# Layer two of a routed pair of expert layers: gathers before the branch, eight weight pieces in flight, three routing rounds

## The chip, the core and the metric

The program runs on one core of a Trainium2 chip. Its compute engines are TensorE (PE, matrix products, whose weight loads the profile lists as PEld), VectorE (DVE), ScalarE (ACT) and GpSimd (POOL); SyncE (SP) issues most DMAs. Each engine works through its own queue in order, and semaphores join the queues. The metric is the device time of one execution in microseconds. The kernel before took 804.73 us, the median of three runs (803.93 to 805.32).

## The reference

Attention with decay gives 2304 tokens of 512 numbers, which pass through two expert layers. In layer one each token goes to its best expert. In layer two the experts fill up: the pairs of token and expert are taken in falling order of their score, and each expert holds exactly 2304 / 8 = 288 tokens.

```python
def _moe2_ref(x, w_gate, w1, w2):
    N, D = x.shape
    E = w_gate.shape[1]
    cap = N // E
    logits = x @ w_gate
    flat = logits.flatten()
    order = np.argsort(-flat)
    assigned = -np.ones(N, dtype=np.int64)
    counts = np.zeros(E, dtype=np.int64)
    for idx in order:
        tok, e = (int(idx) // E, int(idx) % E)
        if assigned[tok] >= 0 or counts[e] >= cap:
            continue
        assigned[tok] = e
        counts[e] += 1
    out = np.zeros((N, D), dtype=np.float32)
    for e in range(E):
        mask = assigned == e
        h = np.maximum(x[mask] @ w1[e], 0.0)
        out[mask] = h @ w2[e]
    return out

def reference(**kwargs):
    ...
    x = attn_out.transpose(0, 2, 1, 3).reshape(B * S, H * D)
    x = _moe_ref(x=x, **moe_kwargs)
    return _moe2_ref(x=x, **moe2_kwargs)
```

## The kernel before

The program is written out in the order in which each engine runs it. Attention comes first, then layer one, its eight experts in falling order of their token counts, then the routing of layer two and its eight experts.

A weight matrix of an expert comes in pieces of 128 x 1024 numbers: pieces 0 to 3 belong to the first product, 4 to 7 to the second. `load` (L853) has SP fetch a piece into a raw tile `wraw`. `upper` (L860) has ACT write its high half `whi`, `lower` (L867) has DVE subtract and write the low half `wlo`, and `split` does both. Products are sums of three: high by high, high by low, low by high. There are four `wraw` buffers, so a fifth load waits until `lower` has read the oldest. `load_next` takes the next piece of the list of all 128.

`Experts.all` (L1624) runs an expert's first product in eight steps (L1574, eight groups of twelve matmuls), its second in four (L1598), and puts other work beside each step in `beside`: the splits of the pieces of the next expert, the gather of its rows (`fetch`, one indirect DMA of POOL per 128 tokens), their transposition (`columns`) and the results of the expert before. A group's sum lies in one of two banks named `pl`; ACT writes its positive part as `room_hh` and DVE the rest as `room_hl` (L1577, L1578), and then the bank is free. The first expert of a layer has nobody before it to prepare its own later pieces, so it splits pieces 4 to 7 in its own steps 0 to 3 (`LATE`).

The class `First` starts the first expert of layer one while attention ends. DVE sorts the experts by their counts in `order_all`, nine short instructions that end with the tile `ordi`, which tells SP which expert's weights to load next.

The class `Clear` routes layer two. Each of the eight experts has a threshold in `c_T`. In a round (L1378) every token chooses the expert with the best score among those whose threshold it passes (`choose`, mask `c_oh`), the margins `c_z` are compared with a grid of 128 steps (`c_cmp`, L1390), twenty matmuls count for each step how many tokens of each expert lie above it (L1395), and the threshold rises by the largest step that leaves 288 (L1396 to L1400). Three rounds run beside the last expert of layer one, on the tokens known by then, dealt out over its steps by the table `SPEC`. Four more run when all scores are there. Then `place` (L1411) turns the choice into the index list `ix`, and computes a flag that is 1 if an expert has not exactly 288 tokens. `run` (L1465) branches on the flag: if it is 1, four more rounds and another placing follow, and if that fails too an exact search. In the traced execution the branch is not taken. After it come the gathers of expert 0, the low halves of its first four pieces with four loads, ten warm-up matmuls, and the transposes (`first_columns`, with matmuls at L890).

Of the kernel before, what the change touches and what calls it, by code (L numbers as in the profile page):

```python
# [289 lines left out]
def attention(tc, ctx, qkT, vrow, vT, f, emb, x_d, identf, identb, psum, R, tau, first_expert):  # L290
# [524 lines left out]
    nc.vector.tensor_reduce(ut, u.rearrange("p k e t -> p e t k"), axis=AX.X, op=ALU.add)  # L815
    for _ in R.order_all():
        pass
    first_expert.last_rows(work)
    first_expert.split(3)
# [26 lines left out]
class Weights:  # L846
# [6 lines left out]
    def load(self, p, j):  # L853
        raw = self.pool.tile([128, 1024], F32, name="wraw", bufs=4)
        e = self.expert(p)
        src = self.w1 if j < 4 else self.w2
        self.nc.sync.dma_start(raw, src[bass.ds(e, 1), j % 4].rearrange("o p x -> (o p) x"))
        self.raw[p, j] = raw

    def upper(self, key, j):  # L860
        pool, k, bufs = (self.pool, "1", 4) if j < 4 else (self.pool2, "2", 8)
        hi = pool.tile([128, 1024], F32R, name="whi" + k, bufs=bufs)
        lo = pool.tile([128, 1024], F32R, name="wlo" + k, bufs=bufs)
        self.nc.scalar.activation(hi, self.raw[key, j], AF.Copy)  # L864
        self.parts[key, j] = (hi, lo)
# [370 lines left out]
ROUNDS = (4, 4)  # L1236

SPEC = {0: 1, 2: 1, 4: 1, 6: 1, 7: 1, 7.5: 5, 9: 1, 9.5: 5, 11: 1, 12: 1}


class Clear:
# [7 lines left out]
    def __init__(self, tc, R, const, work, psum, up, y_d):  # L1249
# [6 lines left out]
        self.oh = self.ohz[:, :, 1:]  # L1256
# [103 lines left out]
    def choose(self, last=False):  # L1360
# [12 lines left out]
        yield  # L1373
        for c in CUT:
            TT(self.oh.rearrange("p e c -> p c e")[:, c], self.V[:, c],
               self.mn[:, c, None].to_broadcast([128, c.stop - c.start, E]), op=ALU.is_equal)

    def round(self, tag="py"):  # L1378
        nc, TT = self.nc, self.nc.vector.tensor_tensor
        yield from self.choose()  # L1380
        ohc = self.oh.rearrange("p e c -> p c e")
        for c in CUT:
            TT(self.V[:, c], ohc[:, c], self.Rm[:, c], op=ALU.mult)
# [3 lines left out]
        h = (0, 14, NCP)  # L1387
# [6 lines left out]
        for c in range(NC3):  # L1394
            nc.tensor.matmul(p, self.cmp[:, :, c], self.oh[:, :, c], start=(c == 0), stop=(c == NC3 - 1))  # L1395
# [18 lines left out]
    def place(self, ix2):  # L1414
# [47 lines left out]
        nc.vector.tensor_scalar(ix2, ut, -1.0, None, op0=ALU.add)  # L1462
        return again[0]

    def run(self, ix2):  # L1465
# [11 lines left out]
        with tc.If(self.place(ix2) > 0):  # L1477
            go(ROUNDS[1])
            with tc.If(self.place(ix2) > 0):
# [6 lines left out]
                self.place(ix2)  # L1486


class Experts:
# [134 lines left out]
    def all(self, load_next, after, extra):  # L1624
# [3 lines left out]
        for p in range(E):  # L1628
# [4 lines left out]
            def beside(step, p=p):  # L1633
# [3 lines left out]
                elif step < 8:  # L1637
# [4 lines left out]
                    if p == 0 and step in LATE:  # L1642
                        W.split(0, 4 + LATE.index(step))
# [10 lines left out]
                elif nW is not None and not last:  # L1654
# [4 lines left out]
        if not self.second:  # L1659
            self.finish(lambda: extra(E - 1, 12))  # L1660

# [18 lines left out]
def moe(tc, ctx, psum, R, later, ut, first_expert, W1, W2, load_next, x_d, wg, out, identf):  # L1680
# [121 lines left out]
    C.run(ix2)  # L1802

    def gather2(p, t, w):
        g = work.tile([128, YW], F32, name="xg", bufs=4)
# [13 lines left out]
    L2.fetch(0)  # L1819
# [84 lines left out]
```

## Time and profile before

| | |
|---|---|
| median of three runs | 804.73 us |
| profiled execution | 805.88 us |
| its span, first to last instruction | 803.7 us |
| busy: PE, PEld, DVE, ACT, POOL | 741.7, 711.0, 498.0, 408.3, 303.3 us |
| mean granted clock of PE | 0.957 |

The profiled execution is a run of its own, and its span leaves out what lies before the first instruction and after the last. Busy times of different engines overlap, so they say which engine is nearly full and not what bounds a stage. The page also cuts the span into 40 slices of 20 us: PE is at 90% or more in all but the first two, four between about 502 and 583 us, and the last. A clock of 1.00 is 2.4 GHz, 0.50 is 1.2 GHz.

### The profile page before, as it was taken

To read this page: it belongs to the slowest core of one execution; us is meant where nothing else is said; L and a number is where in the kernel's file an instruction comes from. 1 tells how busy PE (TensorE), PEld (TensorE's weight loads), DVE (VectorE), ACT (ScalarE), POOL (GpSimd) and SP (SyncE) were. 2 spreads that over 40 slices of the span, in tenths; PEclk is the share of its full clock that TensorE was granted. 3 is DMA by queue.
4 is the path that set the end of the run, shared out by engine and by line. 5 is a ranking of instruction groups with operands and counts; after the bars stand their busy time and mean duration, and the time that the engine had idled before them with its cause. 6 is when DMAs were issued, how large, how long until landed. Compare 5 with 4: busy or idle time off the path is not lost. (4 is left out here: it accounts for less than half of the span.)

```text
span 803.7 us, 16338 instructions
## 1 busy us (share of the span) xinstructions
PE 741.7 (92%) x5813; PEld 711.0 (88%) x5813; DVE 498.0 (62%) x1314; ACT 408.3 (51%) x898; POOL 303.3 (38%) x674
## 2 busy tenths in 40 slices
PE   3799999999999999999999999845899999999995
PEld 1499999999898899999999999723799999999993
DVE  5666887877887676555466567673555555655530
ACT  3456666767657455455555556100555555555420
POOL 5587767777663446423123111004021222232011
PEclk9799999999999999999999999855899999999998
DMA  5456766767664556455565562004546655665310
GB/s 124 92 122 153 168 152 164 161 157 174 143 198 131 170 175 194 149 182 175 168 192 180 185 183 84 26 1 168 174 171 197 211 171 195 209 194 175 124 37 31
DMA packets 70254, 121.74 MB, mean 151 GB/s; under 512 B 29498, under 2 KB 38714, under 8 KB 70164
## 3 DMA queue, kind: packets, MB, share of 16 engines
q1 hardware_dynamic: 63924, 101.24, 45.5%
q0 software_dynamic: 6240, 19.36, 6.4%
q8 instruction: 50, 0.82, 0.4%
q14 instruction: 40, 0.33, 0.1%
HBM read 96.46 MB, written 14.63 MB: 138 GB/s over the span
## 5 line engine op out<-in xcount | busy, mean ns | idle before, releaser
L870 DVE TENSOR_TENSOR wlo<-wraw,whi 128x1024 fp32r<-128x1024 f32 x128 | 156.3, 1227 | 126.4 <-ACT whi L864 122.0
L864 ACT ACTIVATE whi<-wraw 128x1024 fp32r<-128x1024 f32 x128 | 134.6, 1056 | 3.6 <-DMA wraw<-v 3.2
L477 POOL TENSOR_TENSOR opB<-raw,opA 64x576 fp32r<-64x576 f32 x64 | 90.7, 1417 | 34.3 <-ACT opA L473 31.6
L1577 ACT ACTIVATE room_hh<-pl 128x288 fp32r<-128x288 f32 (+8 forms) x128 | 51.9, 406 | 97.9 <-PE pl L1574 94.4
L1574 PE MATMUL pl<-room_xh,whi 128*128 128x288 f32 (+7 forms) x512 | 94.9, 308 | 4.5 <-DVE room_hl L1578 4.4
L1574 PE MATMUL pl<-room_xl,whi 128*128 128x288 f32 (+7 forms) x512 | 90.6, 299 | 0.0
L1574 PE MATMUL pl<-room_xh,wlo 128*128 128x288 f32 (+7 forms) x512 | 90.5, 299 | 0.0
L1598 PE MATMUL py<-room_hh,wlo 128*128 128x288 f32 (+7 forms) x480 | 89.8, 310 | 0.0
L1578 DVE SCALAR_TENSOR_TENSOR room_hl<-pl,room_hh 128x288 fp32r<-128x288 f32 (+8 forms) x128 | 57.3, 448 | 52.0 <-ACT room_hh L1577 50.4
L1574 PEld LDWEIGHTS pl<-room_xh,whi 128*128 128x128 f32 x512 | 76.4, 192 | 6.1 <-DVE room_hl L1578 5.6
L1574 PEld LDWEIGHTS pl<-room_xl,whi 128*128 128x128 f32 x512 | 76.8, 191 | 0.0
L1574 PEld LDWEIGHTS pl<-room_xh,wlo 128*128 128x128 f32 x512 | 76.7, 191 | 0.0
L1806 POOL DMA_INDIRECT xg<-y_d,ix x24 | 29.2, 1219 | 125.2 <-PE px L1514 89.9
L1598 PE MATMUL py<-room_hh,whi 128*128 128x288 f32 (+7 forms) x480 | 75.9, 300 | 0.0
L1598 PE MATMUL py<-room_hl,whi 128*128 128x288 f32 (+7 forms) x480 | 75.8, 300 | 0.0
L513 PE MATMUL pl<-opA 96*128 96x288 f32 (+2 forms) x192 | 67.5, 356 | 7.0 <-DVE opA L382 3.7
L549 PE MATMUL px<-opA 128*128 128x288 f32 (+2 forms) x192 | 72.2, 376 | 0.0
L1598 PEld LDWEIGHTS py<-room_hh,wlo 128*128 128x128 f32 x480 | 70.5, 189 | 0.0
L582 PE MATMUL py<-vv,room_hh 128*128 128x73 f32 x480 | 69.7, 265 | 0.4 <-DVE vv L497 0.4
L517 DVE CUSTOM_DVE_ANT_0 mxs<-pl,mask 128x512 f32<-128x512 f32 (+3 forms) x128 | 61.9, 484 | 13.1 <-PE pl L513 9.7
L1598 PEld LDWEIGHTS py<-room_hl,whi 128*128 128x128 f32 x480 | 69.1, 188 | 0.0
L1598 PEld LDWEIGHTS py<-room_hh,whi 128*128 128x128 f32 x480 | 69.0, 189 | 0.0
(367 smaller groups left out, 1417.4 us busy)
## 6 DMA issues: line engine op xcount, KB each, us to landing
wraw<-w SPq DMA_DIRECT2D x64, 512.0 KB, 4.1
wraw<-v SPq DMA_DIRECT2D x64, 512.0 KB, 3.5
raw<-qkT SPq DMA_DIRECT2D x32, 288.0 KB, 4.3
opB<-opA SPq DMA_DIRECT2D x64, 144.0 KB, 3.1
vv<-vrow SPq DMA_DIRECT2D x32, 160.0 KB, 4.6
vt<-vT SPq DMA_DIRECT2D x16, 288.0 KB, 4.4
x_d<-xr SPq DMA_DIRECT2D x16, 256.0 KB, 2.7
opA<-chl SPq DMA_DIRECT2D x60, 2.2 KB, 1.8
```

The source lines that it names most:

```text
L477: nc.gpsimd.tensor_tensor(b_[lo, t, :], raw[:, t, :], r32(a[0:64, t, :]), op=ALU.subtract)
L513: nc.tensor.matmul(p[:, :wp], af[0:96, q0:q0 + 128], a[0:96, 1, k0:k0 + wp], start=True, stop=True)
L517: nc.vector.tensor_tensor_reduce(t[:qw, :w], p[:qw, :w], mask[:qw, m0:m0 + w], 1.0, part4[:qw] if i == 4 else -3.0e38, op0=ALU.add, op1=AL ...
L549: nc.tensor.matmul(o, af[:, ks], a[:, 0, q1 - wp:q1], start=True, stop=False)
L582: nc.tensor.matmul(p[:, i, :], PT[n % 2][0][:, c:c + 128], v_[:, j, :], start=(k == 0), stop=(k == len(AORD) - 1))
L864: self.nc.scalar.activation(hi, self.raw[key, j], AF.Copy)
L870: self.nc.vector.tensor_tensor(lo, self.raw.pop((key, j)), r32(hi), op=ALU.subtract)
L1574: nc.tensor.matmul(o, a[:, d, f0:f0 + 128], b[:, d, o0:C], start=(n == 0), stop=(n == 11))
L1577: nc.scalar.activation(hh[:, fc, c0:C], o, AF.Relu)
L1578: nc.vector.scalar_tensor_tensor(hl[:, fc, c0:C], o, 0.0, r32(hh[:, fc, c0:C]), op0=ALU.max, op1=ALU.subtract)
L1598: nc.tensor.matmul(o, a[:, fc, :], b[:, fc, :C], start=(n == 0), stop=(n == 23))
L1806: nc.gpsimd.indirect_dma_start(out=g[:w], out_offset=None, in_=y_d, in_offset=IOA(ap=ix2[:w, p * NT + t:p * NT + t + 1], axis=0))
```

## The change

Five things change.

The first expert's fourth piece is split ahead of `order_all` and not behind it.

Pieces 4 to 7 get raw buffers of their own, four tiles `wraw2`, so eight pieces can be on their way. Their high and low tiles go from eight buffers to six. The first expert of layer one calls `load_next` twice in each of its steps 0 to 3. For the first expert of layer two, ACT writes the high halves of pieces 4 to 7 while layer one ends (two beside the last expert's second product, two behind its last evictions), and only the low halves are left for its own steps.

After the scores are complete, three rounds run and not four. A branch that is taken still has four.

Inside a round the mask goes to a tile of its own, `c_ohc`, in the order token, expert, and only the last choice is written to `c_oh`, in the order expert, token, which `place` reads. The comparison is made in three pieces of 8, 6 and 6 columns and not in two of 14 and 6, so `SPEC` has one more step per round.

The gathers of expert 0 are issued behind `place` and ahead of the branch. The branch's body ends with a copy of them (`again`). An index is now at least 0.

```diff
@@ -813,10 +813,10 @@
+    first_expert.split(3)
     for _ in R.order_all():
         pass
     first_expert.last_rows(work)
-    first_expert.split(3)
     first_expert.load_next()
@@ -851,14 +851,15 @@
     def load(self, p, j):
-        raw = self.pool.tile([128, 1024], F32, name="wraw", bufs=4)
+        pool, k = (self.pool2, "2") if self.pool2 and j > 3 else (self.pool, "")
+        raw = pool.tile([128, 1024], F32, name="wraw" + k, bufs=4)
...
     def upper(self, key, j):
-        pool, k, bufs = (self.pool, "1", 4) if j < 4 else (self.pool2, "2", 8)
+        pool, k, bufs = (self.pool, "1", 4) if j < 4 else (self.pool2, "2", 6)
@@ -1233,9 +1234,9 @@
-ROUNDS = (4, 4)
-
-SPEC = {0: 1, 2: 1, 4: 1, 6: 1, 7: 1, 7.5: 5, 9: 1, 9.5: 5, 11: 1, 12: 1}
+ROUNDS = (3, 4)
+
+SPEC = {0: 1, 2: 1, 4: 1, 5: 1, 6: 1, 7: 1, 7.5: 6, 9: 1, 9.5: 6, 11: 1, 12: 1}
@@ -1253,7 +1254,7 @@
-        self.oh = self.ohz[:, :, 1:]
+        self.oh, self.ohc = self.ohz[:, :, 1:], t(sh, BF, "c_ohc")
@@ -1371,20 +1372,20 @@
+        oh = self.oh.rearrange("p e c -> p c e") if last else self.ohc
         for c in CUT:
-            TT(self.oh.rearrange("p e c -> p c e")[:, c], self.V[:, c],
+            TT(oh[:, c], self.V[:, c],
                self.mn[:, c, None].to_broadcast([128, c.stop - c.start, E]), op=ALU.is_equal)
...
-            TT(self.V[:, c], ohc[:, c], self.Rm[:, c], op=ALU.mult)
+            TT(self.V[:, c], self.ohc[:, c], self.Rm[:, c], op=ALU.mult)
...
-        h = (0, 14, NCP)
+        h = (0, 8, 14, NCP)
@@ -1392,7 +1393,7 @@
-            nc.tensor.matmul(p, self.cmp[:, :, c], self.oh[:, :, c], start=(c == 0), stop=(c == NC3 - 1))
+            nc.tensor.matmul(p, self.cmp[:, :, c], self.ohc[:, c], start=(c == 0), stop=(c == NC3 - 1))
@@ -1459,10 +1460,10 @@
-        nc.vector.tensor_scalar(ix2, ut, -1.0, None, op0=ALU.add)
+        nc.vector.tensor_scalar(ix2, ut, -1.0, 0.0, op0=ALU.add, op1=ALU.max)
...
-        with tc.If(self.place(ix2) > 0):
+        flag = self.place(ix2)
+
+        fetch()
+        with tc.If(flag > 0):
             go(ROUNDS[1])
...
+            again()
@@ -1640,7 +1645,11 @@
                     if p == 0 and step in LATE:
-                        W.split(0, 4 + LATE.index(step))
+                        if self.cold:
+                            W.upper(0, 4 + step)
+
+                            load_next()
+                        W.lower(0, 4 + step)
                         load_next()
@@ -1651,13 +1660,18 @@
-                elif nW is not None and not last:
+                elif last:
+                    if step in (9, 11):
+                        nW.upper(np_, 4 + step // 10)
+                elif nW is not None:
...
             self.finish(lambda: extra(E - 1, 12))
+            for j in (6, 7):
+                nW.upper(np_, j)
@@ -1816,7 +1830,7 @@
-    L2.fetch(0)
+    C.run(ix2, lambda: L2.fetch(0), lambda: [gather2(0, t, w, L2.rows[0][t]) for t, w in L2.tiles(0)])
```

The order on three engines shows where instructions went. First DVE, where attention ends; `tk_u` is the last tile of the token search, `order` and `ordi` the sorted experts, `wlo` the low half of the fourth piece, and `room_hl` the next thing that PE's product gives it. Before:

```order
L815 TENSOR_REDUCE tk_u<-px 128x24
L171 TENSOR_TENSOR cnt<-pl_carry,base 128x8
L173 SCALAR_TENSOR_TENSOR o_key_3920<-cnt,ev 128x8
L175 SCALAR_TENSOR_TENSOR o_key_3920<-fh,o_key_3920 128x8
L177 TENSOR_TENSOR o_m<-o_key_3920 128x64
L179 TENSOR_REDUCE o_pos<-o_m 128x8
L181 TENSOR_TENSOR perm<-ev,o_pos 128x64
L190 TENSOR_TENSOR o_m<-perm,ev 128x64
L192 TENSOR_REDUCE order<-o_m 128x8
L186 CAST ordi<-order 1x8
L870 TENSOR_TENSOR wlo_3938<-wraw,whi_3937 128x1024
L984 SCALAR_TENSOR_TENSOR room_hl<-pl,room_hh 128x256
```

Now:

```order
L815 TENSOR_REDUCE tk_u<-px 128x24
L871 TENSOR_TENSOR wlo_3920<-wraw,whi_3919 128x1024
L171 TENSOR_TENSOR cnt<-pl_carry,base 128x8
L173 SCALAR_TENSOR_TENSOR o_key_3924<-cnt,ev 128x8
L175 SCALAR_TENSOR_TENSOR o_key_3924<-fh,o_key_3924 128x8
L177 TENSOR_TENSOR o_m<-o_key_3924 128x64
L179 TENSOR_REDUCE o_pos<-o_m 128x8
L181 TENSOR_TENSOR perm<-ev,o_pos 128x64
L190 TENSOR_TENSOR o_m<-perm,ev 128x64
L192 TENSOR_REDUCE order<-o_m 128x8
L186 CAST ordi<-order 1x8
L985 SCALAR_TENSOR_TENSOR room_hl<-pl,room_hh 128x256
```

The low half has passed the nine instructions of the sort, and `room_hl` follows the sort directly.

Next POOL at the branch. `DMASW` names the semaphores of POOL's DMAs. Before, the gathers of expert 0 stand behind the branch's end:

```order
L1479 UNCONDITIONAL_BRANCH [waits Pool_49,Pool_sequencer_49]
L1477 UNCONDITIONAL_BRANCH [waits Pool_49,Pool_sequencer_49]
L1806 DMA xg<-y_d,ix_7677 128x520 [waits DMASW2_49,DMASW4_49,DVE_49,PE_49]
L1806 DMA xg<-y_d,ix_7677 128x520 [waits PE_49]
L1806 DMA xg<-y_d,ix_7677 32x520 [waits DMASW3_49,PE_49]
L1825 COPY ix_8657<-ix_7677 32x1
```

Now they stand ahead of it, and the branch's end, on the path that skips the body, has an instruction that waits for three DMA semaphores:

```order
L1820 DMA xg<-y_d,ix_7701 128x520 [waits DMASW2_49,DMASW4_49,DVE_49,PE_49]
L1820 DMA xg<-y_d,ix_7701 128x520 [waits PE_49]
L1820 DMA xg<-y_d,ix_7701 32x520 [waits DMASW3_49,PE_49]
L1481 COMPARE_AND_BRANCH
L1460 TENSOR_LOAD c_bi [waits DVE_49]
```

```order
L1481 UNCONDITIONAL_BRANCH
L1481 ISA [waits Pool_49,Pool_sequencer_49,DMASW2_49,DMASW1_49,DMASW0_49]
L1481 UNCONDITIONAL_BRANCH
L1839 COPY ix_7702<-ix_7701 32x1 [waits DVE_49]
L1839 COPY ix_7702<-ix_7701 32x1 [waits Pool_49]
L1839 COPY ix_7702<-ix_7701 32x1 x5
L1820 DMA xg<-y_d,ix_7701 128x520 [waits DMASW3_49,PE_49]
```

The three gathers have passed the comparison, and the copies and the gathers of expert 1 stand behind the new wait. PE's transposes of the gathered rows wait for two semaphores a tile now, one of the gather and one of its copy in the body:

```order
L891 MATMUL px<-identf,xg 128x128 [waits DMASW5_49,DMASW0_49]
L891 MATMUL px<-identf,xg 128x128 [waits DVE_49,PE_49]
L891 MATMUL py<-identf,xg 128x128 x2
L891 MATMUL px<-identf,xg 128x128 [waits DMASW6_49,DMASW1_49]
L891 MATMUL px<-identf,xg 128x128
L891 MATMUL py<-identf,xg 128x128 x2
L891 MATMUL px<-identf,xg 128x128 [waits DMASW7_49,DMASW2_49]
```

Last ACT in the first product of layer two's expert 0, where `whi` is the high half of a weight piece. Before:

```order
L1577 ACTIVATE room_hh<-pl 128x288
L864 ACTIVATE whi_8743<-wraw 128x1024
L1577 ACTIVATE room_hh<-pl 128x288
L864 ACTIVATE whi_8764<-wraw 128x1024
L864 ACTIVATE whi_8770<-wraw 128x1024
L1577 ACTIVATE room_hh<-pl 128x288
L864 ACTIVATE whi_8791<-wraw 128x1024
L1577 ACTIVATE room_hh<-pl 128x288
L864 ACTIVATE whi_8812<-wraw 128x1024
L864 ACTIVATE whi_8818<-wraw 128x1024
```

Now:

```order
L1582 ACTIVATE room_hh<-pl 128x288 x2
L865 ACTIVATE whi_8759<-wraw 128x1024
L1582 ACTIVATE room_hh<-pl 128x288 x2
L865 ACTIVATE whi_8801<-wraw 128x1024
L1582 ACTIVATE room_hh<-pl 128x288 x2
L865 ACTIVATE whi_8837<-wraw 128x1024
L1582 ACTIVATE room_hh<-pl 128x288 x2
L865 ACTIVATE whi_8873<-wraw 128x1024
```

The four high halves of expert 0's own pieces are gone from between the evictions, and one of expert 1's stands behind every second eviction.

## Rows read from the trace of the kernel before

**Rows 1.** Windows: us, then busy us (x instructions) of PE, PEld, DVE, ACT, POOL; PEclk; DMA.
```profile
268.00:511.00 243.00, 242.51 (x1829) 241.05 (x1828) 149.38 (x340) 133.12 (x260) 71.68 (x335) 1.00 0.53 166
511.00:582.00 71.00, 43.07 (x282) 34.78 (x282) 42.26 (x119) 13.04 (x25) 11.27 (x16) 0.66 0.31 103
```

**Rows 2.** Timeline around 262 us (start, us, engine, line, operation, tiles, idle before and releaser).
```profile
261.29 1.65 DVE L870 TENSOR_TENSOR wlo<-wraw,whi 128x1024 fp32r<-128x1024 f32 x1
263.00 0.74 PE L974 MATMUL pl<-room_xh,wlo 128*128 128x256 f32 x4 [2.35 <-DVE wlo L870]
264.26 0.42 DVE L984 SCALAR_TENSOR_TENSOR room_hl<-pl,room_hh 128x256 fp32r<-128x256 f32 x1 [1.32 <-ACT room_hh L978]
264.63 0.46 DVE L894 TENSOR_TENSOR room_xl<-px,room_xh 128x112 fp32r<-128x112 f32 x2
```

**Rows 3.** Windows: four stretches with the granted clock (PEclk).
```profile
264.00:268.00 4.00, 4.00 (x24) 4.00 (x23) 2.22 (x8) 1.27 (x6) 0.00 (x0) 0.57 0.37 130
268.00:272.00 4.00, 3.94 (x34) 3.74 (x33) 2.58 (x6) 3.15 (x6) 2.56 (x2) 1.00 0.24 66
553.00:564.00 11.00, 6.08 (x24) 5.01 (x24) 2.24 (x5) 1.32 (x4) 6.29 (x13) 0.50 0.75 269
574.00:578.00 4.00, 4.00 (x22) 4.00 (x21) 3.73 (x5) 1.82 (x3) 0.00 (x0) 0.61 0.79 197
```

**Rows 4.** Timeline of one round and its end, DVE and PE.
```profile
525.56 0.39 DVE L1364 TENSOR_TENSOR c_R<-c_L,c_T 128x80 f32<-128x80 f32 x2
526.47 0.87 DVE L1375 TENSOR_TENSOR c_oh<-c_V,c_mn 128x80 bf16<-128x80 f32 x2
527.01 0.64 DVE L1383 TENSOR_TENSOR c_V<-c_oh,c_R 128x80 f32<-128x80 bf16 x2
...
529.13 1.38 PE L1395 MATMUL py<-c_oh,c_cmp 128*128 128x8 bf16 x20 [3.80 <-DVE c_cmp L1390]
...
536.77 0.39 DVE L1364 TENSOR_TENSOR c_R<-c_L,c_T 128x80 f32<-128x80 f32 x2
```

**Rows 5.** Groups by line and form, 514 to 537 us: busy us, mean ns, idle before.
```profile
L1390 DVE TENSOR_TENSOR c_cmp<-c_z,c_G 128x1792 bf16<-128x1792 bf16 x4 | 4.4, 1094 | 0.1
L1390 DVE TENSOR_TENSOR c_cmp<-c_z,c_G 128x768 bf16<-128x768 bf16 x4 | 2.3, 575 | 0.0
```

**Rows 6.** Timeline from the new index to expert 0 of layer two.
```profile
545.89 0.18 DVE L1462 TENSOR_SCALAR ix<-c_ut 128x24 int32<-128x24 f32 x1
...
548.92 4.45 PE L287 MATMUL pl<-identb 128*128 128x512 bf16 x10 [3.30 <-DVEq L1477]
549.06 4.63 DVE L870 TENSOR_TENSOR wlo<-wraw,whi 128x1024 fp32r<-128x1024 f32 x4 [2.99 <-DVEq L1477]
...
559.40 0.69 PE L890 MATMUL px<-identf,xg 128*128 128x128 f32 x2 [3.75 <-DMA xg<-y_d,ix]
...
561.23 1.51 PE L1574 MATMUL pl<-room_xh,whi 128*128 128x288 f32 x4
...
570.91 1.06 ACT L864 ACTIVATE whi<-wraw 128x1024 fp32r<-128x1024 f32 x1 [3.18 <-DMA wraw<-v]
...
573.65 0.81 PE L1574 MATMUL pl<-room_xh,whi 128*128 128x288 f32 x4 [3.98 <-DVE room_hl L1578]
...
579.54 0.69 PE L1574 MATMUL pl<-room_xh,wlo 128*128 128x288 f32 x4
...
580.08 0.69 PE L1574 MATMUL pl<-room_xh,whi 128*128 128x288 f32 x4
...
581.67 1.23 PE L1598 MATMUL py<-room_hh,whi 128*128 128x288 f32 x8
```

**Rows 7.** Tile xg, 540 to 600 us: duration ns min/median/max, first and last start us.
```profile
L1806 POOL DMA_INDIRECT xg<-y_d,ix x9: 862/954/1925, 549.7 to 596.3; - x9
...
DMA to landing us min/median/max: 3.4/3.6/4.8
```

**Rows 8.** The page, costliest groups: busy us, mean ns, idle before.
```profile
L1578 DVE SCALAR_TENSOR_TENSOR room_hl<-pl,room_hh 128x288 fp32r<-128x288 f32 (+8 forms) x128 | 57.3, 448 | 52.0 <-ACT room_hh L1577 50.4
```

More of the change, by code (lines that the diff above doesn't have):

```diff
@@ L1380, in round @@
         yield from self.choose()
-        ohc = self.oh.rearrange("p e c -> p c e")
         for c in CUT:
-            TT(self.V[:, c], ohc[:, c], self.Rm[:, c], op=ALU.mult)
+            TT(self.V[:, c], self.ohc[:, c], self.Rm[:, c], op=ALU.mult)
         with nc.allow_low_precision(reason="only one term is not zero, and the steps leave room"):
@@ L1461, in place, with run @@
         nc.vector.tensor_reduce(ut, u.rearrange("p k e t -> p (e t) k"), axis=AX.X, op=ALU.add)
-        nc.vector.tensor_scalar(ix2, ut, -1.0, None, op0=ALU.add)
+        nc.vector.tensor_scalar(ix2, ut, -1.0, 0.0, op0=ALU.add, op1=ALU.max)
         return again[0]
-    def run(self, ix2):
+    def run(self, ix2, fetch, again):
         nc, tc, R, work, psum = self.nc, self.tc, self.R, self.work, self.psum
@@ L1801, in moe, with gather2 @@
     ix2 = const.tile([128, T], I32, name="ix2")
-    C.run(ix2)
-    def gather2(p, t, w):
-        g = work.tile([128, YW], F32, name="xg", bufs=4)
+    def gather2(p, t, w, g=None):
+        if g is None:
+            g = work.tile([128, YW], F32, name="xg", bufs=4)
         nc.gpsimd.indirect_dma_start(out=g[:w], out_offset=None, in_=y_d,
```

## The prediction

> **What bounds the kernel now.** I read the busy shares by stage first, then who waited for whom inside the stage that is not full, then that stage's instructions in order of time. From 268 to 511 us TensorE (PE) is busy 242.5 of 243 us at clock 1.00, while from 511 to 582 us it works 43 of 71 us at a mean clock of 0.66 [rows 1]. Nothing the change does to an already full PE can shorten it, so what counts is that second stretch and one hole before 268 us. The hole: PE waits 2.35 us for `wlo`, the low half of the first expert's fourth weight piece, which VectorE (DVE) starts only at 261.29 [rows 2]. The second stretch is the routing of layer two, then the start of its first expert. The routing runs on DVE and PE in turn, in rounds of (536.77 - 525.56) / 2 = 5.60 us [rows 4]. Then every engine passes a branch: the index `ix` is done at 546.07, DVE goes on 2.99 us later, PE's warm-up matmuls start at 548.92, and the rows of the first expert are transposed in full only from 559.40 on, after a wait of 3.75 us for the gather. The expert's first product starts at 561.23, stops until 573.65, and its second product starts at 581.67 [rows 6].
>
> The sum is made against the profiled execution, 805.88 us; the median of the runs shown is 1.15 us below it, and I subtract the same there.
>
> **A. The fourth piece's split ahead of the order.** The same ten DVE instructions run in another order: `wlo` first, then the nine that sort the experts. PE's 2.35 us go [rows 2]. After that wait PE ran at a granted clock of 0.57 from 264 to 268 us, 24 matmuls, against 34 in the next four us at 1.00 [rows 3]; 24 at the faster rate take 2.8 us, so 1.2 more go if the clock stays up. What is late next: the DVE block still ends at 262.94 (261.29 + 1.65), and behind it stand a 0.42 us `room_hl` and two pairs of `room_xl` of 0.46 us [rows 2], so the last `room_xl` comes at about 264.2. PE, going on at 260.65 (263.00 - 2.35), needs it after three us of products, at about 263.6. That gives back 0.6. A = 2.35 + 1.2 - 0.6 = 3.0; bounds 1.8 (clock falls all the same) and 3.6. The sorted order, now later by a split, is wanted only by the loads of expert 1, by SyncE (SP).
>
> **B. Three rounds, shorter ones.** One round less is 5.60 [rows 4]. In the other three the choice's mask goes to a dense tile. Before, the pair of mask writes holds DVE 0.54 us (526.47 to 527.01), while the three pairs before it take 0.91 together, 0.30 each: 0.23 less if the dense write costs what they do. The pair that reads the mask is busy 0.64 against 0.39: 0.25 less [rows 4]. No row shows a dense mask of 16-bit numbers; the ends are nothing and this 0.48, and I take it whole, since output shape and count are those of the 0.39 pair. The comparison goes from pieces of 14 and 6 columns to 8, 6 and 6. Its two forms take 1.094 and 0.575 us [rows 5], so 0.065 a column and 0.186 fixed: 8 columns take 0.705 and the first matmul may start 0.39 earlier. The third piece adds about 0.1 to DVE, and the last six of twenty matmuls (1.38 us for all, [rows 4]) then wait a little: 0.35 is left. A round is 5.60 - 0.23 - 0.25 - 0.35 = 4.77. B = 4 x 5.60 - 3 x 4.77 = 8.1; bounds 5.3 (layout gives nothing, the third piece costs 0.1 a round) and 8.6. The three rounds beside the last expert of layer one lie under a full PE.
>
> On the mask's layout the Trainium skill has a rule (SBUF — State Buffer, section "Door 1: The DMA port swizzle", the note on cachelines): accesses that stay in a 16-byte line run at full rate, each step to a new line costs. Before, two experts of a token lie 42 bytes apart, afterwards eight lie in 16 bytes. By the rule the 0.48 us a round all goes; were the mixed number types the cause instead, none would, and B would be 6.6. The rows show the slower pair but not why.
>
> **C. Rows gathered ahead of the branch.** The gathers wait for `ix` alone now, and start at about 546.2 (on the clock of before). An unhindered one takes 0.95 us on GpSimd (POOL) [rows 7], with a gap of some 0.3: the third starts at 548.7 and lands 3.6 us later [rows 7], at 552.3. The change adds a wait: on the path not taken POOL first waits for all three to land, then raises the semaphores that the copy of the gathers in the branch would have raised, and PE's transposes wait for those. Behind it on POOL stand the small index copies and the gathers of the next expert, which nobody wants for 15 us. PE meanwhile does its ten warm-ups (548.92 + 4.45 = 553.4, [rows 6]), so these decide. Twelve transposes at clock 0.50 [rows 3] follow at once; the eight from 559.40 on took 1.83 to the first product, so twelve take 2.7 less the overlap, and the product starts at about 555.9 instead of 561.23. C = 5.3; bounds 2.7 (second rival) and 6.7 (the clock rises before the transposes).
>
> **D. Eight weight pieces on their way.** Before, ScalarE (ACT) stood 3.18 us at 570.91 for a raw piece of expert 1 that had no buffer earlier, and PE's 3.98 us until 573.65 came from that, ACT's queue being in order [rows 6]. Now pieces 4 to 7 of expert 0 have their high halves written behind the last evictions of layer one, and expert 1's first four load right after the branch, 9 us before they are wanted. So that stall goes. What is late next is DVE. The first product has eight groups of 12 matmuls, 3 x 0.54 = 1.6 us each at full clock (579.54 to 580.08, four matmuls, [rows 6]), and group n + 2 needs the bank that group n's `room_hl` frees. Beside groups 0 to 3 DVE has four `room_hl` of 0.45 [rows 8] and six low halves of 1.16 (4.63 / 4, [rows 6]), 8.8 us against PE's 6.4. Going through the two queues PE waits some 1.0 us before group 4 and 1.3 before group 6. 8 x 1.6 + 2.3 + 1.4 (the first group at half clock) = 16.5 us, against 581.67 - 561.23 = 20.4. D = 3.9; bounds 2.9 and 5.4. The 16 extra loads in flight during layer one are the same bytes, earlier; the high and low tiles of the second product, six instead of eight, are taken again only after the product that read them.
>
> **Sum.** 3.0 + 8.1 + 5.3 + 3.9 = 20.3: 805.88 - 20.3 = 785.6 in a profiled execution, 784.4 as the median. The end of layer two has nothing new in it.
>
> **The rivals.** *Three rounds are not enough* (slower). The flag is raised as soon as one expert does not have exactly 288 tokens after six rounds, three of them on incomplete tokens; then four more rounds (19.1), the last choice and the placing again (546.07 - 536.77 = 9.3) and two passages of a branch (3.0 each) follow, 34 us: 818. For it: the trace shows that seven rounds suffice, not that six do. Against it: the rounds worked out from the reference's numbers leave 88 tokens too many or too few after one full round, 16 after two and 0 after three, and relative errors of 1e-5 in the logits leave the 0. Chance 0.03.
>
> *The merge is late.* If POOL's jump and the wait behind the gathers let the transposes start as long after the first gather as before (559.40 - 549.7 = 9.7, [rows 6, 7]), they start at 556.0, not 553.4: 787.0. For it: DVE's branch took 2.99 us, and the weight loads begin as POOL jumps. The Trainium skill (Runtime: NRT & Kernel Launch, section on instruction fetch) says that a taken branch out of the fetched window waits for a DMA fetch of its target; that would put POOL's jump behind these loads. Chance 0.10.
>
> *The clock falls again.* DVE's two waits of a us, or the 0.6 in A, bring the half clock back for four us; 22 matmuls ran in such a stretch at 574 [rows 3]: 1.2 lost twice, and 0.6: 787.4. Chance 0.10.
>
> *The dense mask and the third piece give nothing* (that part doesn't do what it says): B is 5.3, 787.2. Chance 0.10.
>
> **How the numbers follow.** The forecast as summed has 0.66, the last 0.01 is a loss elsewhere that eats all. All rivals but the first stay within five us; adding the low ends of B, C and D against the high ends gives 779.5 to 789.5 for 8 in 10. This kernel's measurement tells about 0.2% (1.6 us) from no change: faster 0.96, within it 0.01, slower 0.03.
>
> **What would show it.** A: no PE wait on `wlo` near 260 us, a short one on `room_xl` in its place, clock 1.00 after. B: three rounds at 4.8 us, the branch's body not run, the mask pair at 0.3 us. C: gathers before the warm-ups, transposes directly behind them at about 7.3 us after `ix`. D: no ACT wait for `wraw` in expert 0, PE waits of about a us on `room_hl`, the second product some 16 us after the first. A second set of rounds, or transposes more than 9 us after `ix`, would make the forecast wrong.

## The result, and the profile after

The changed kernel takes 782.76 us as the median of four runs (781.61 to 784.40); the kernel before, on the same chip, 805.03 (803.93 to 806.37). The ratio is 0.972, 95% interval 0.970 to 0.975. The forecast was 784.4, in a range of 779.5 to 789.5. The profiled execution took 784.4 us against a predicted 785.6, with a span of 782.7 us.

To see where the 21.0 us of span went, I cut both spans at five marks that every kernel of this study has: the last `lp` of the attention on DVE, before any changed code; the first full round of layer two (`c_R`); the end of `ix`; the start of the first product of expert 0 of layer two; the start of its second product. All times are differences of start times in the timelines, in us.

| stage | before | after | gain | forecast |
|---|---|---|---|---|
| last `lp` to first full round (A) | 264.09 | 260.65 | 3.44 | 3.0 |
| first full round to end of `ix` (B) | 31.79 | 23.85 | 7.94 | 8.1 |
| end of `ix` to first product (C) | 15.16 | 9.73 | 5.43 | 5.3 |
| first to second product (D) | 20.44 | 15.20 | 5.24 | 3.9 |
| second product to the end | 222.03 | 222.43 | -0.40 | 0 |

The five gains make 21.65. The mark itself came 0.65 later in the profiled execution after (250.84 against 250.19), in work that is the same in both, which leaves 21.0. The last row is no loss of time: from the start of the second product to the last store that POOL issues it is 213.20 us before and 213.13 after. Only the end of the span comes 0.4 us later behind that store, and in return 1.7 us of the profiled execution lie outside the span and not 2.2, so that its time fell by 21.5.

The windows of the changed kernel that answer to [rows 1] and [rows 3] (us, then busy us of PE, PEld, DVE, ACT and POOL with their instructions, granted clock of PE, DMA share, GB/s):

```profile
264.00:268.00 4.00, 4.00 (x36) 4.00 (x35) 2.94 (x9) 2.45 (x4) 1.28 (x2) 1.00 0.00 0
268.00:511.00 243.00, 242.20 (x1828) 240.45 (x1827) 146.82 (x344) 132.40 (x259) 69.01 (x334) 1.00 0.55 175
511.00:560.00 49.00, 33.60 (x229) 26.34 (x229) 35.31 (x102) 11.14 (x22) 12.87 (x16) 0.76 0.41 128
```

From 264 to 268 us PE now runs 36 matmuls at clock 1.00, where there were 24 at 0.57. The middle is as full as it was. By the marks, the stretch from the first full round to the second product (B to D) has gone from 67.4 to 48.8 us; the windows of 71 and 49 us are cut more roughly.

The place of [rows 2], the end of the first expert's first product in layer one, in the timeline of PE and DVE:

```profile
257.42 1.22 DVE L871 TENSOR_TENSOR wlo<-wraw,whi 128x1024 fp32r<-128x1024 f32 x1
...
263.11 0.16 DVE L186 CAST ordi<-order 1x8 int32<-1x8 f32 x1
263.19 0.42 DVE L985 SCALAR_TENSOR_TENSOR room_hl<-pl,room_hh 128x256 fp32r<-128x256 f32 x1
...
263.75 0.72 PE L1579 MATMUL pl<-room_xh,whi 128*128 128x256 f32 x4 [0.19 <-DVE room_hl L985]
```

The low half stands ahead of the sort now, and PE no longer waits for it. What is left there is a wait of 0.19 us for a `room_hl` that follows the sort.

A round, in the timeline of DVE and PE, to be held against [rows 4]:

```profile
521.43 0.39 DVE L1365 TENSOR_TENSOR c_R<-c_L,c_T 128x80 f32<-128x80 f32 x2
...
522.34 0.38 DVE L1377 TENSOR_TENSOR c_ohc<-c_V,c_mn 128x80 bf16<-128x80 f32 x2
522.64 0.38 DVE L1384 TENSOR_TENSOR c_V<-c_ohc,c_R 128x80 f32<-128x80 bf16 x2
...
523.97 1.51 PE L1396 MATMUL py<-c_ohc,c_cmp 128*128 128x8 bf16 x20 [2.77 <-DVE c_cmp L1391]
...
526.13 0.39 DVE L1365 TENSOR_TENSOR c_R<-c_L,c_T 128x80 f32<-128x80 f32 x2
```

The round lasts 4.70 us (before 5.60); the two mask pairs take 0.38 us each (before 0.87 and 0.64), and PE waits 2.77 us for the comparison (before 3.80).

From the index to the first product, PE and POOL, to be held against [rows 6]:

```profile
536.16 1.00 POOL L1820 DMA_INDIRECT xg<-y_d,ix  x1 [17.82 <-DVE ix L1463]
537.47 0.96 POOL L1820 DMA_INDIRECT xg<-y_d,ix  x1 [0.30 <-POOLq L1481]
538.30 3.95 PE L287 MATMUL pl<-identb 128*128 128x512 bf16 x10 [3.42 <-DVEq L1481]
538.73 1.70 POOL L1820 DMA_INDIRECT xg<-y_d,ix  x1 [0.30 <-DMA y_d<-yrow,six]
540.43 3.56 POOL L1839 COPY ix<-ix 32x1 int32<-32x1 int32 x7
542.09 0.38 PE L891 MATMUL px<-identf,xg 128*128 128x128 f32 x2
...
544.27 0.41 PE L891 MATMUL px<-identf,xg 128*128 128x128 f32 x2 [1.14 <-DMA xg<-y_d,ix]
...
545.07 1.31 PE L1579 MATMUL pl<-room_xh,whi 128*128 128x288 f32 x4 [0.17 <-ACT room_xh L894]
...
560.27 1.23 PE L1603 MATMUL py<-room_hh,whi 128*128 128x288 f32 x8
```

`ix` ends at 535.34. The gathers start 0.82 us later, ahead of the branch, and the transposes follow directly on the warm-ups, 6.75 us after `ix`. The third tile alone is late.

Who PE waited for from 500 to 570 us (total, times, longest), the largest rows:

```profile
PE py L1396 <- DVE c_cmp L1391: 5.5, 2, 2.8
PE pl L287 <- DVEq L1481: 3.4, 1, 3.4
PE pl L200 <- DVE c_big L1427: 2.2, 1, 2.2
PE px L891 <- DMA xg<-y_d,ix: 1.1, 1, 1.1
PE pl L1579 <- DVE room_hl L1583: 1.1, 2, 0.7
```

The stop of 3.98 us inside the first product is gone. In its place stand two short ones, 0.45 us before the fifth group and 0.67 before the seventh.

### The profile page after: what moved, and what is told of

It reads as the page before. It is cut to its first block, busy times and chain, and to the rows that moved or that the text cites. A ratio compares the mean times of both kernels' runs of the same rounds, so it can differ in the third digit from the quotient of the medians.

```text
span 782.7 us, 16284 instructions
## 1 busy us (share of the span) xinstructions
PE 733.7 (94%) x5792; PEld 704.7 (90%) x5792; DVE 490.4 (63%) x1304; ACT 408.3 (52%) x898; POOL 305.1 (39%) x674
## 5 line engine op out<-in xcount | busy, mean ns | idle before, releaser
L871 DVE TENSOR_TENSOR wlo<-wraw,whi 128x1024 fp32r<-128x1024 f32 x128 | 155.8, 1223 | 123.3 <-ACT whi L865 118.8
L582 PE MATMUL py<-vv,room_hl 128*128 128x73 f32 x480 | 68.9, 266 | 0.0
```

The costliest lines, as they stand in the source:

```text
L582: nc.tensor.matmul(p[:, i, :], PT[n % 2][0][:, c:c + 128], v_[:, j, :], start=(k == 0), stop=(k == len(AORD) - 1))
L871: self.nc.vector.tensor_tensor(lo, self.raw.pop((key, j)), r32(hi), op=ALU.subtract)
```

## The experiments

Each kernel is the changed one with one thing altered, unless it says otherwise. Whole runs of one kernel spread over up to 3.5 us (781.61 to 784.40 for the changed kernel; up to 6.2 for the kernel before), so small effects are read from the stages, of one trace per kernel. The experiments ran in further sessions, in which the kernel before took 805.6 to 806.2 us. The stages of all profiled executions, cut as above:

| kernel | A | B | C | D | to the end | ratio to before, interval |
|---|---|---|---|---|---|---|
| before | 264.09 | 31.79 | 15.16 | 20.44 | 222.03 | |
| after | 260.65 | 23.85 | 9.73 | 15.20 | 222.43 | 0.972 (0.970 to 0.975) |
| u_split | 264.01 | 23.92 | 9.38 | 15.20 | 222.40 | 0.976 (0.972 to 0.981) |
| u_rounds | 260.16 | 28.41 | 9.66 | 15.91 | 222.39 | 0.977 (0.973 to 0.982) |
| u_mask | 260.41 | 24.91 | 9.70 | 15.77 | 222.42 | 0.973 (0.969 to 0.977) |
| u_pieces | 260.13 | 24.55 | 9.52 | 15.84 | 222.45 | 0.973 (0.968 to 0.977) |
| u_gather | 260.70 | 23.71 | 15.97 | 16.53 | 221.97 | 0.980 (0.978 to 0.981) |
| u_again | 260.70 | 23.85 | 9.80 | 15.21 | 221.94 | 0.973 (0.970 to 0.975) |
| u_weights | 260.61 | 23.93 | 9.50 | 20.48 | 222.43 | 0.979 (0.977 to 0.981) |
| w_warm6 | 260.29 | 23.69 | 9.28 | 16.50 | 222.41 | 0.973 (0.970 to 0.975) |
| b_rounds | 264.03 | 26.11 | 14.12 | 20.50 | 222.01 | 0.993 (0.991 to 0.995) |
| n_low5 | 260.18 | 23.78 | 9.78 | 15.19 | 222.40 | 0.971 (0.969 to 0.973) |
| n_even | 260.66 | 23.96 | 9.62 | 14.61 | 222.42 | 0.971 (0.969 to 0.974) |
| n_even5 | 260.17 | 23.34 | 9.95 | 14.32 | 222.42 | 0.970 (0.968 to 0.973) |

Column by column it shows that each part of the change acts in its own stage; C and D alone are joined, by the clock. Two differences come from somewhere else.

Stage D is 15.77 to 15.91 us in u_rounds, u_mask and u_pieces, which do not alter it. There the second `room_hh` of the product, on ACT, starts 0.6 to 0.8 us behind the end of its group's matmuls, and in the changed kernel 0.05 behind it (those ends are 549.18 in the changed kernel and 553.11 in u_rounds), and the fourth and fifth groups of the product start late. The timeline of ACT in the changed kernel, then in u_rounds:

```profile
549.23 0.41 ACT L1582 ACTIVATE room_hh<-pl 128x288 fp32r<-128x288 f32 x1 [1.13 <-PE pl L1579]
```

```profile
553.89 0.41 ACT L1582 ACTIVATE room_hh<-pl 128x288 fp32r<-128x288 f32 x1 [1.86 <-PE pl L1579]
```

n_even and n_even5 have the same delay. No row shows its cause, and whether it belongs to these kernels or to the executions that were traced is open.

The last column is 222.39 to 222.45 us in the ten kernels with a copy of the gathers in the branch's body, and 221.94 to 222.03 in the four without. It is the place of the span's end that moves, as said above: 1.7 to 1.9 us of the profiled execution lie outside the span in the ten, 2.1 to 2.2 in the four.

**u_split**: the fourth piece's split behind the sort again.

```diff
-    first_expert.split(3)
     for _ in R.order_all():
         pass
     first_expert.last_rows(work)
+    first_expert.split(3)
```

> The changed kernel with the first expert's fourth piece split behind the sort again. Theory (four waits that add up): the PE wait of 2.35 us on the low half is back near 260 us, the granted clock falls to 0.50 for about three us behind it, and the kernel takes 3.0 to 3.8 us more than the changed one: about 786.3. Rival (the gain came from the earlier weight loads that layer one now has, not from the split): below 784, with no wait of 2 us.

Stage A is 264.01 again, 3.4 us longer, and no other stage moves by more than 0.4. The rival, that earlier weight loads made the gain, is out. Its timeline of PE and its windows show the wait and the clock after it:

```profile
262.79 0.74 PE L975 MATMUL pl<-room_xh,wlo 128*128 128x256 f32 x4 [2.32 <-DVE wlo L871]
```

```profile
264.00:268.00 4.00, 4.00 (x24) 4.00 (x22) 2.38 (x9) 1.12 (x5) 0.00 (x0) 0.57 0.31 123
```

So the part is worth its wait of 2.3 us and a further 1.1, which are 24 matmuls instead of 36 in four us at the granted clock of 0.57. The median of this kernel is 787.27 us, 0.976 of before and a us above what was expected.

**u_rounds**: four rounds, short ones.

```diff
-ROUNDS = (3, 4)
+ROUNDS = (4, 4)
```

> The changed kernel with four rounds after the scores are complete and not three. Theory: one round of the new length more, 4.7 us, nothing else moved: 787.5. Rival (the round removed overlapped with the stores of layer one's last rows, which then set the start of the gathers): less than 3 us.

Stage B grows by 4.56 us, so the rival (less than 3) is out, and the added round lasts 4.70, as the timeline of DVE shows. The whole, 788.57 us, is 1.1 above what was expected; 0.7 of it stand in stage D.

```profile
525.36 0.39 DVE L1365 TENSOR_TENSOR c_R<-c_L,c_T 128x80 f32<-128x80 f32 x2
...
530.06 0.39 DVE L1365 TENSOR_TENSOR c_R<-c_L,c_T 128x80 f32<-128x80 f32 x2
```

**u_mask**: the rounds write and read the strided mask again; number types, shapes and pieces are as after.

```diff
-        oh = self.oh.rearrange("p e c -> p c e") if last else self.ohc
+        oh = self.oh.rearrange("p e c -> p c e")
```

(and the two readers of `self.ohc` in `Clear` read `self.oh`).

> The changed kernel with the mask of every round in the strided tile again, three pieces kept. Theory (layout sets the price): the pair that writes the mask takes 0.87 us and the pair that reads it 0.64, a round is 0.48 us longer, 1.4 us in all: 784.2. Rival (mixed number types set the price, the layout nothing): both pairs stay at 0.38 and the time is that of the changed kernel.

**u_pieces**: the dense mask, but the comparison in two pieces.

```diff
-        h = (0, 8, 14, NCP)
+        h = (0, 14, NCP)
```

(and the table of steps beside layer one's last expert, `SPEC`, drops a step in each of three places).

> The changed kernel with the comparison in two pieces of 14 and 6 columns again, the dense mask kept. Theory: the matmuls of a round start 0.39 us later and a round is 0.35 us longer, 1.0 us in all: 783.8. Rival (the third piece costs as much as its earlier start gives): no difference, a round of 4.7 us.

A round takes 5.21 us with the strided mask and 5.09 with two pieces, against 4.70. The timelines of DVE and PE in u_mask, then of PE in u_pieces:

```profile
521.82 0.87 DVE L1377 TENSOR_TENSOR c_oh<-c_V,c_mn 128x80 bf16<-128x80 f32 x2
522.37 0.64 DVE L1384 TENSOR_TENSOR c_V<-c_oh,c_R 128x80 f32<-128x80 bf16 x2
...
523.95 1.52 PE L1396 MATMUL py<-c_oh,c_cmp 128*128 128x8 bf16 x20 [3.27 <-DVE c_cmp L1391]
```

```profile
523.79 1.37 PE L1396 MATMUL py<-c_ohc,c_cmp 128*128 128x8 bf16 x20 [3.29 <-DVE c_cmp L1391]
```

In u_mask the two pairs are back at 0.87 and 0.64 us, and the number types have not been touched, so the layout was the cause. The Trainium skill (SBUF — State Buffer, section "Door 1: The DMA port swizzle") says that accesses which stay in a 16-byte line run at full rate; this case agrees, with 0.51 us a round for 160 strided 16-bit numbers in a partition, written and read. Over the stage the two undone parts cost 1.06 and 0.70 us. That is less than three times a round's difference, because the first full round gains nothing: it lasts 5.25 us in the changed kernel, where its counting matmuls start 0.30 us behind the last results of layer one, and 5.22 and 5.10 in these two. The medians, 785.01 and 784.76 us, are 2.2 and 2.0 above the changed kernel's, where 1.4 and 1.0 were expected; stage D's 0.6 is part of that. The intervals of the ratios tell neither from the changed kernel.

**u_gather**: the gathers stand behind the branch again.

```diff
-    C.run(ix2, lambda: L2.fetch(0), lambda: [gather2(0, t, w, L2.rows[0][t]) for t, w in L2.tiles(0)])
+    C.run(ix2, lambda: None, lambda: None)
+    L2.fetch(0)
```

> The changed kernel with the gathers of layer two's expert 0 behind the branch again. Theory: as before the change they meet the four weight loads, the transposes of the second tile start about 13 us after the index and the first product some 15 us after it, 4 to 5.4 us later than in the changed kernel: 787 to 788. Rival (with eight pieces in flight the loads no longer hold the gathers up, so C was really a gain of the weight buffers): at most 2 us later.

Stage C is 15.97 us, 6.2 longer, and stage D, in which nothing was altered, 16.53, 1.3 longer. The rival (at most 2 us) is out, and the median, 789.62 us, lies above the 787 to 788 expected: C lost more than was thought, and the loss in D was not in the sum. The timeline of PE, then a window:

```profile
549.17 0.69 PE L891 MATMUL px<-identf,xg 128*128 128x128 f32 x2 [4.94 <-DMA xg<-y_d,ix]
...
551.00 1.51 PE L1579 MATMUL pl<-room_xh,whi 128*128 128x288 f32 x4
552.31 1.16 PE L1579 MATMUL pl<-room_xl,whi 128*128 128x288 f32 x4
...
555.19 0.74 PE L1579 MATMUL pl<-room_xl,whi 128*128 128x288 f32 x4
```

```profile
550.00:554.00 4.00, 4.00 (x18) 3.69 (x17) 1.55 (x4) 1.32 (x4) 1.83 (x2) 0.50 0.22 47
```

After the idle 4.94 us PE is granted 0.50 of its clock (1.2 of 2.4 GHz): the first sixteen matmuls of the product take 4.2 us, where sixteen take 2.1 later on. The gathers ahead of the branch are therefore worth 6.2 us before the product and 1.3 inside it.

**u_again**: the branch's body has no copy of the gathers, so POOL has no semaphores to make up for on the path not taken. (The body is not run in either kernel; if it were, its rows would be stale.)

```diff
-    C.run(ix2, lambda: L2.fetch(0), lambda: [gather2(0, t, w, L2.rows[0][t]) for t, w in L2.tiles(0)])
+    C.run(ix2, lambda: L2.fetch(0), lambda: None)
```

> The changed kernel without the copy of the gathers in the branch's body, which also takes away the wait at the branch's end (the body, not run here, would leave the rows of the first index). Theory: the ten warm-ups decide when the first transposes start, and the landing of the third gather decides the last of them, so the first product starts within 0.5 us of 9.7 us after the index and the time is the same within 0.6 us: 782.2 to 783.4. Rival (the merge on GpSimd costs what the third tile waits for): the wait of 1.1 us before the third tile goes and the kernel is 1 us faster: 781.7.

No stage moves but the span's end: the product starts 9.80 us after `ix` (9.73 with the copy), and its third gather takes 1.65 us on POOL (1.70) and lands 5.5 us after its start (5.4). The added wait costs nothing, and the late third tile doesn't come from it. PE's 1.1 us ahead of that tile do go here, as in the rival, but for another reason and with no gain: the warm-ups take 4.45 us and not 3.95, the transposes start 7.15 us after `ix` and not 6.75, and they reach the third tile when it lands.

**u_weights**: the weight tiles are pooled and split as before, so expert 0 comes with four high halves written.

```diff
-        pool, k = (self.pool2, "2") if self.pool2 and j > 3 else (self.pool, "")
+        pool, k = self.pool, ""
...
-                        if self.cold:
-                            W.upper(0, 4 + step)
-
-                            load_next()
-                        W.lower(0, 4 + step)
+                        W.split(0, 4 + step)
```

(`bufs` of the second pool goes from 6 to 8, and the four early `upper` calls go.)

> The changed kernel with the weights as before: four raw buffers, eight high and low tiles, the four high halves made in expert 0's own steps, one load in each. Theory: ScalarE waits for a raw piece again in expert 0, TensorE stops about 4 us, and the first product takes 19 to 20.4 us and not 15.2: 787 to 788. Rival (the stall came from the late gathers and has gone with them): the first product takes at most 16.5 us, 784 or less.

Stage D is 20.48 us again, and nothing else changes, so the rival (the stall went with the late gathers) is out; the median is 788.78 us, 0.8 above what was expected. The separate buffers and the early high halves were undone together, and which of them is worth how much isn't shown. The timelines of ACT and PE have the pair of waits of [rows 6] back:

```profile
552.88 1.06 ACT L865 ACTIVATE whi<-wraw 128x1024 fp32r<-128x1024 f32 x1 [3.28 <-DMA wraw<-v]
...
555.62 1.33 PE L1579 MATMUL pl<-room_xh,whi 128*128 128x288 f32 x4 [4.02 <-DVE room_hl L1583]
556.74 1.17 PE L1579 MATMUL pl<-room_xl,whi 128*128 128x288 f32 x4
557.70 1.17 PE L1579 MATMUL pl<-room_xh,wlo 128*128 128x288 f32 x4
```

The clock falls behind this wait too (0.50 from 556 to 559 us): four matmuls take 0.96 us from one row to the next, where they take 0.53 at full clock.

**w_warm6**: six warm-up matmuls instead of ten after the branch.

```diff
-WARM = (8, 8, 15, 3, 6, 10)
+WARM = (8, 8, 15, 3, 6, 6)
```

> The changed kernel with six warm-up matmuls behind the branch and not ten. Theory (warm-ups decide the first transposes, the third gather the last): the first transposes start up to 1.7 us earlier, the third tile's not, the first product starts within 0.3 us of where it did, but at the slow clock if the clock is still low by then, up to 1.5 us lost: 782.8 to 784.3. Rival (the warm-ups decide all): 1.6 us faster: 781.2.

The transposes start 5.44 us after `ix` instead of 6.75, but the third tile is waited for all the same (1.35 us), so the product starts only 0.45 earlier (at most 0.3 was expected), and stage D is 1.3 longer. The rival (warm-ups decide all) is out. The timeline of PE, and two windows of each kernel (w_warm6 first, then after):

```profile
543.29 0.41 PE L891 MATMUL px<-identf,xg 128*128 128x128 f32 x2 [1.35 <-DMA xg<-y_d,ix]
...
546.36 1.17 PE L1579 MATMUL pl<-room_xh,wlo 128*128 128x288 f32 x4
```

```profile
542.00:546.00 4.00, 2.54 (x11) 1.98 (x12) 1.89 (x5) 1.32 (x4) 3.06 (x8) 0.86 0.92 328
546.00:550.00 4.00, 4.00 (x24) 4.00 (x23) 1.59 (x2) 0.85 (x3) 1.79 (x2) 0.72 0.85 301
```

```profile
542.00:546.00 4.00, 2.68 (x18) 1.81 (x16) 2.03 (x4) 1.32 (x4) 3.34 (x7) 1.00 0.91 315
546.00:550.00 4.00, 4.00 (x30) 3.89 (x30) 2.41 (x5) 1.19 (x3) 2.21 (x3) 1.00 0.92 335
```

With ten warm-ups the clock is 1.00 when the product starts; with six it is at 0.72 during it. What the shorter queue wins, the clock takes back.

**b_rounds**: the kernel before with three rounds for layer two, and nothing else.

```diff
-ROUNDS = (4, 4)
+ROUNDS = (3, 4)
```

> The kernel before with only layer two's routing at three rounds instead of four, with its strided mask and two pieces, and nothing else of the change. Theory (a round is worth what it lasts there, 5.6 us, and nothing behind it moves): three full rounds are left, indices 5.6 us earlier, stages behind as before (15.2 and 20.4 us), the whole about 799.4. Rival (three rounds do not fix the choice for this layer, so the slow way is run): over 810. Other rival (the weights of the first expert, in flight meanwhile, are late when the routing is shorter): under 4 us of gain, with a longer stage of the first product.

800.10 us against 806.11: a ratio of 0.993 and stage B 5.68 us shorter, one round of that kernel (5.60 to 5.67 between the starts of its rounds). The choice is fixed after three rounds and the branch's body not run. Stage D stays at 20.50: a shorter routing alone doesn't make the weights late or early. Stage C is also 1.0 us shorter in this execution, in which PE waits 3.22 us for the later gathers and not 3.75; why is not shown.

**n_low5**: the fifth low half ahead of the transposes, too.

```diff
-    for j in range(4):
+    for j in range(5):
         W2.lower(0, j)
```

(and step 0 of `beside` skips it in layer two).

> The changed kernel with a fifth low half of layer two's first expert subtracted ahead of the branch (the fifth weight tile's), so that the gap in which the gathers land does more of the splitting. In the changed kernel TensorE waits 0.45 and 0.67 us for room_hl inside the first product, behind VectorE's subtractions. Theory (VectorE's low halves are what the first product still waits for): both waits go or shrink, the first product's stage falls from 15.2 to 14.1 to 14.6 us, and the whole to about 782. Rival (the fifth subtraction of 0.45 us stands in the queue of VectorE ahead of the transposes' copies and of the gather's neighbours): the first product begins that much later after the indices, 10.2 against 9.7 us, and the whole stays within 0.5 us of 782.8.

The theory fell. DVE's five subtractions (the fifth takes 1.13 us, not 0.45) end before the transposes' copies are wanted, so the rival's delay isn't there, but the two waits are 0.44 and 0.67 us as before. The time won stands as idle time on DVE ahead of the second `room_hl`. So less work for DVE ahead of its pairs of subtractions does not shorten PE's waits.

**n_even**: the same low halves, one behind each eviction instead of two behind every second one.

```diff
-                    if p == 0 and step in LATE:
+                    if p == 0 and (step in LATE if self.cold else step in (0, 2, 4, 6)):
...
-                        W.lower(0, 4 + step)
+                        W.lower(0, 4 + (step if self.cold else step // 2))
```

> The changed kernel with the low halves inside layer two's first product put one behind each eviction, on VectorE, instead of two behind every second one (same instructions, another order). Taking one subtraction out of the product ahead of it (n_low5) left TensorE's two waits at 0.44 and 0.67 us, so the sum of VectorE's work does not set them. Theory (the pair does: two subtractions, 2.35 us, stand ahead of an eviction's low half that a bank waits for, and a product group lasts 1.6): one subtraction and one room_hl are 1.17 + 0.45 = 1.6 us a group, just what TensorE takes, so both waits go or fall under 0.2 us, the stage from first to second product goes from 15.2 to 14.0 to 14.4 us, and the whole to about 782 against 782.8. Rival (the waits come from ScalarE's high half ahead of room_hh, not from VectorE's order): waits stay at a sum of 1.0 or more, the stage at 15.2.

**n_even5**: both.

> As n_even, and the fifth low half ahead of the transposes as in n_low5. Theory of the pair: VectorE has one group's slack more, no wait on room_hl is left, stage 13.9 to 14.3 us, the whole 781.5 to 782.3. Rival (fully packed VectorE shifts the wait to the second product's low halves instead): no wait in the first product but a new one of up to a us in the second, stage times no shorter in sum.

The timeline of DVE in the changed kernel, where a pair of low halves stands ahead of the `room_hl` whose bank the fifth group needs, and the one of n_even:

```profile
550.06 2.35 DVE L871 TENSOR_TENSOR wlo<-wraw,whi 128x1024 fp32r<-128x1024 f32 x2
552.33 0.45 DVE L1583 SCALAR_TENSOR_TENSOR room_hl<-pl,room_hh 128x288 fp32r<-128x288 f32 x1
```

```profile
551.48 0.45 DVE L1583 SCALAR_TENSOR_TENSOR room_hl<-pl,room_hh 128x288 fp32r<-128x288 f32 x1
551.85 1.22 DVE L871 TENSOR_TENSOR wlo<-wraw,whi 128x1024 fp32r<-128x1024 f32 x1
552.98 0.45 DVE L1583 SCALAR_TENSOR_TENSOR room_hl<-pl,room_hh 128x288 fp32r<-128x288 f32 x1
```

PE's waits for `room_hl` in the first product fall from 1.1 to 0.5 us in n_even and to 0.2 in n_even5, by the rows of waits:

```profile
PE pl L1579 <- DVE room_hl L1583: 0.5, 2, 0.3
```

```profile
PE pl L1579 <- DVE room_hl L1583: 0.2, 1, 0.2
```

So the order was the cause of the waits, and stage D is 14.61 and 14.32 us, just above what was expected. What is left of the waits stands behind the late second `room_hh`, here in the timeline of ACT in n_even:

```profile
548.95 0.41 ACT L1582 ACTIVATE room_hh<-pl 128x288 fp32r<-128x288 f32 x1 [2.04 <-PE pl L1579]
```

It starts 0.95 us behind the end of its group in n_even and 0.65 in n_even5, and DVE stands idle ahead of the `room_hl` that follows it in both. These 0.30 us are the whole difference between the two stages, so no gain of the fifth low half is shown. The new wait in the second product that n_even5's rival wanted is not there: the last column is unchanged. As whole runs the two take 782.99 and 782.26 us. n_even5 is the shortest of all kernels here and beats the kernel before by 23 us, but its half us over the changed kernel lies within the scatter of runs: only the traces show the shorter stage.

## Why the prediction was right, step by step

**A** was 3.4 us instead of 3.0, against the kernel before and against u_split; in the kernels with the early split the stage itself spreads over 0.6. The wait and the clock were as said. The term that was too big is what it gave back: 0.6 was taken for a late `room_xl`, and the wait that came is 0.19 for `room_hl`. PE takes `room_xh` first and reads `room_xl` only from 264.31 on, without a wait.

**B** was 7.94 against 8.1, with a round of 4.70 against 4.77. The parts hold singly: the layout is worth 0.51 us a round (forecast 0.48) and the pieces 0.39 (0.35). What the sum missed is the first full round, which lasts 5.25 in this execution because its matmuls stand behind the last work of layer one. In n_even5, where PE waits there for the comparison, it lasts 4.72.

**C** was 5.43 against 5.3, but by another way, and that it came so near is luck. I let twelve transposes run at half clock behind the warm-ups and all gathers land before them. But the third gather started 3.4 us after `ix` and not 2.6, and landed 5.4 us after its start instead of 3.6, so that the third tile and not the warm-ups decided when the product starts. The clock rose during the warm-ups, so the transposes took half the time, and PE waited 1.14 us for the tile. The two errors cancel. In u_rounds, u_mask, u_again and n_even5 the warm-ups took 4.4 us, at half clock, as I had it, and the product started 9.66 to 9.95 us after `ix` all the same. u_again excludes the merge as the cause of the late landing. That rival (the merge is late) is out: the transposes came 6.75 us after `ix`, not over 9.

**D** is the term that was mis-sized: 5.24 against 3.9. The stall went, as u_weights shows by bringing it back. Two prices of the new product were too high. The waits on `room_hl`, at the very groups named, are 1.1 us in all and 1.65 with the slower restarts behind them, and not 2.3; DVE's ten instructions beside the first four groups take 8.3 us from the first start to the end of the last (548.19 to 556.47) and not 8.8. And the start costs 0.75 us and not 1.4, because C leaves PE busy and at full clock: eight groups of 1.6 us, 1.65 and 0.75 make the 15.2. With C undone the stage is 16.53 us, the 16.5 that I had worked out, yet even that sum was right only by two errors against each other, since the cold start costs 2.1 us there and not 1.4 and the waits 1.6 and not 2.3.

**The rivals.** That three rounds don't suffice is excluded by every run with three. The clock did not fall again (1.00 from 545 to 560 us). Mask and pieces give what was said. The unchanged rest, forecast at nothing, cost nothing: the 0.4 us in the table are the place of the span's end, not time.

## What to carry to other kernels

When two parts of a change lie one behind the other, the first one's end state is the second one's start: whether TensorE arrives busy or idle was worth 1.3 us to a product that was itself untouched. A start that waits for two things moves only with the one that comes last: transposes that began 1.3 us earlier brought the product forward by 0.45. A wait that an in-order engine causes is mended by the order of its work before its amount: one subtraction less changed nothing, and the same subtractions spread evenly took the waits from 1.1 to 0.5 us. And a small operation that is repeated in a chain is worth its layout: a mask laid dense gave half a us a round.

## What the runs showed of the hardware beyond the forecast

- POOL's work is slower while DVE runs its long subtractions (L871). The third gather's issue takes 1.70 us beside them and 0.95 alone; seven index copies take 3.56 us beside them in the changed kernel and 1.52 in u_gather, where they start at 543.58 and DVE is busy for only 0.69 of the four us around. With a fifth subtraction ahead of the transposes (n_low5, n_even5) the copies take 4.49, 0.93 more. That points at the subtractions; how they slow POOL was not tried.
- The third gather lands 5.4 us after its start, where an unhindered one took 3.6 [rows 7]; the weight loads of expert 1 start a us after it, at 539.75. In u_gather the slowest takes 8.7. Whether it is these loads or POOL's slow issue stays open.
- DVE idles 2.87 to 3.19 us at the branch in all traces (3.10 in the changed kernel, 2.99 before), whatever else was changed.
